# The third 2-byte part of q and k: from a product with minus the identity on TensorE to a subtraction on GpSimd

## The chip, the cores and the metric

The kernel runs on one core of a Trainium2 chip. The metric is the device time of one execution in microseconds (us); lower is better. The kernel before takes 673.02 us, the median of three runs (672.89 to 673.35). PE stands for TensorE, DVE for VectorE, ACT for ScalarE, POOL for GpSimd, SP for SyncE, the engine whose queue issues most DMAs.

## What is computed

Two independent computations stand side by side in one output of 2048 x 1152. Half A is attention with a compressive memory over a 2048 x 576 input, 32 heads of 18, in four segments of 512 rows. Half B filters another 2048 x 576 input in the frequency domain.

```python
# half A
q, k, v = heads(x @ wq), heads(x @ wk), heads(x @ wv)      # 32 heads of 18, N = 4 segments of L = 512
for s in range(4):
    p = softmax(qs @ ks.T * scale + causal_mask)
    a_mem = (phi(qs) @ M) / (phi(qs) @ z + 1e-6)           # phi(t) = t + 1 if t > 0 else exp(t)
    outs.append(g * a_mem + (1 - g) * (p @ vs))
    M, z = M + phi(ks).T @ vs, z + phi(ks).sum(rows)
a = concat(outs) @ wo
# half B
b = irfft2(rfft2(x) * (w_r + 1j * w_i))
```

All of it is 4-byte arithmetic in the reference. The kernel gets near that on TensorE by splitting an operand into a high part and the remainder; for the scores of the attention it holds each of q and k as a sum of three 2-byte numbers.

## The kernel before

Four stages follow one another on TensorE: the forward transform of half B (to about 67 us), the projections of half A (about 67 to 274 us), the inverse transform of half B (about 274 to 347 us), and the attention. The middle of half B, its small transforms across slices and its multiplication by the filter, is elementwise work on DVE. It is cut into steps of one instruction or half an instruction, and a pacer issues a given number of these steps between the pieces of the projections (`pace.take`). There is no scheduler that reorders: every engine runs its instructions in the order in which the code issues them, and waits at each for its inputs and its buffers.

**The projections** (`projections`) run over the four segments g. Each segment has 13 units: nine units of q and k (`qk_unit`, mt = 0 to 8, here q0 to q8; mt < 4 holds q rows, mt = 4 a mixture, mt > 4 k rows) and four of v (`v_unit`, v0 to v3). A q unit is 14 products of 128x128 by 128x512 into one PSUM bank named `pj` (L487). A v unit is two banks of 14 products with 288 columns; in the first three segments five small products per v unit (`pm`), issued some steps later, add up the memory matrix. The tag `pj` has five banks, shared by both kinds. A unit is a generator: its passes are issued in its own turn of the loop, and its later steps in the turns of the units behind it, two steps in each turn (`advance`), the older unit first.

**The steps of a q unit**, after its passes, with the lines of the kernel before:

1. ACT writes the first 2-byte part `sp3[:,j0]` from `pj` (L500). Where phi is needed, ACT also makes exp(min(t,0)) in tile `ex` (L503, L504).
2. DVE makes phi in `ex` (L506, with one operand in PSUM and one in SBUF), and subtracts the first part from `pj` in place (L507).
3. ACT writes the second part from `pj` (L514).
4. PE multiplies minus the identity (`nid`, 2-byte) with the second part and adds it to `pj` (L516): what is left in the bank is the third part, which ACT copies out (L517). SP stores the three parts to DRAM (L520, L521; for mt = 4 six DMAs, L526), and PE transposes phi of k (L533).
5. ACT copies the transposes into `pk` (L536, L537).

Step 1 of a unit stands right behind step 3 of the unit before it in ACT's order, so that per unit ACT runs L514, L500, L503, L504, L517. The tile `sp3` has three buffers; L500 of a unit waits until the stores of the third unit before it have landed. `vt`, the tile of 622 columns into which ACT copies v (L551), has two buffers; POOL writes its columns of ones (L548, L549), SP stores it (L552), and `pm` reads it (L559).

**DVE's other work there**: the steps of half B (L232, L244, L267, L270, L274, L276), which read two operands from SBUF and write SBUF, the remainders of the inputs and weights (L431, L460, L466), which do too, and the masking of the memory matrix from PSUM (L567). In the last segment DVE also makes the split `Y` (L305) of the first two units of the inverse transform, of which the first products after the projections (L320) read. POOL does little in this stage: memsets, the sums of the memory matrix (L572 to L576), and in the last segment the issue of the DMAs for the tables of the inverse transform (L285, L286, L291), which waits until the last q unit has released the weights.

Of the kernel before, what the change touches and what calls it, by code (L numbers as in the profile page):

```python
# [5 lines left out]
F32=mybir.dt.float32; F32R=mybir.dt.float32r  # L6
AF=mybir.ActivationFunctionType; OP=mybir.AluOpType
# [358 lines left out]
BF=mybir.dt.bfloat16  # L366
# [43 lines left out]
class ATT:  # L410
# [78 lines left out]
    def qk_unit(s,g,mt,tp,pp):  # L489

        nc=s.nc
        ps=pp.tile([128,512],F32,name="pj",tag="pj")
        yield from s.passes(ps,g,"wqk",slice(128*mt,128*mt+128),slice(0,512),False)
        yield
        sp3=tp.tile([128,3,512],BF,name="sp3",bufs=3)
        r0=0 if (g>0 or mt>4) else 64
        r1=128 if (g<3 or mt<4) else 64
        if (g==0 and mt<4) or (g==3 and mt>4): r1=r0
        j=[2,1,0] if mt>4 else [0,2,1] if mt<4 else [0,1,2]
        nc.scalar.copy(sp3[:,j[0]],ps)  # L500
        if r1>r0:
            e=tp.tile([128,512],F32,name="ex")
            nc.scalar.activation(e[r0:r1],ps[r0:r1],AF.Relu,scale=-1.0)  # L503
            nc.scalar.activation(e[r0:r1],e[r0:r1],AF.Exp,scale=-1.0)  # L504
        yield
        if r1>r0: nc.vector.scalar_tensor_tensor(e[r0:r1],ps[r0:r1],0.0,e[r0:r1],op0=OP.max,op1=OP.add)  # L506
        nc.vector.tensor_tensor(ps,ps,sp3[:,j[0]],op=OP.subtract)  # L507
        qr=min(r1,128 if mt<4 else (64 if mt==4 else 0))
        if qr>r0:
            a=s.pqD[g][0]  # L510
            J=[(18*8*mt*512,[[512,16],[18*512,8]],e[:qr])] if mt<4 else [((16+j)*512,[[18*512,32]],e[32*j:32*j+32]) for j in range(2)]
            for o,ap,x in J: nc.sync.dma_start(bass.AP(tensor=a.tensor,offset=a.offset+o,ap=ap+[[1,512]]),x)
        yield
        nc.scalar.copy(sp3[:,j[1]],ps)  # L514
        yield
        nc.tensor.matmul(ps,s.nid,sp3[:,j[1]],start=False,stop=True,skip_group_check=True)  # L516
        nc.scalar.copy(sp3[:,j[2]],ps)  # L517
        if mt!=4:
            d=s.qkD[g][mt-(mt>4)]; o=mt<4
            nc.sync.dma_start(d[o:o+3].rearrange("i p c -> p i c"),sp3)  # L520
            nc.sync.dma_start(d[3-3*o],sp3[:,1-o])  # L521
        else:
            for r,i,c,n in ((0,0,1,3),(0,1,1,2),(0,2,1,1),(64,0,3,3),(64,0,2,2),(64,0,1,1)):
                m={3:0,2:3,1:5}[n]; a=s.reD[g][r*12//64+2*m]
                x=sp3[r:r+64,i:i+c] if c==n else sp3[r:r+64,i:i+1].to_broadcast([64,n,512])
                nc.sync.dma_start(bass.AP(tensor=a.tensor,offset=a.offset,ap=[[512,64],[64*512,n],[1,512]]),x)  # L526
        if r1<=r0: return
        k0=max(r0,0 if mt>4 else (64 if mt==4 else 128))
        if k0>=r1: return
        n=r1-k0  # L530
        pt=pp.tile([128,4,128],F32,name="ptr",tag="pt")
        for tb in range(4):
            nc.tensor.transpose(pt[:,tb,:n],e[k0:r1,128*tb:128*tb+128],s.ident[k0:r1,k0:r1])  # L533
        yield
        pk=s.pk.rearrange("p a (h d) -> p a h d",d=18)
        if mt==4: nc.scalar.copy(pk[:,:,:,16:],pt[:,:,:n].rearrange("p a (d h) -> p a h d",d=2))  # L536
        else: nc.scalar.copy(pk[:,:,8*mt-40:8*mt-32,:16],pt.rearrange("p a (d h) -> p a h d",h=8))  # L537
    def v_unit(s,g,tb,tp,pp):
        nc=s.nc
        P=[]  # L540
# [36 lines left out]
    def projections(s,xp,tp,pp,wv,pace,hook):  # L577

        live=[]
        s.nid=wv.tile([128,128],BF,name="nid"); s.nc.scalar.activation(s.nid,s.ident,AF.Copy,scale=-1.0)  # L580
        lw=s.load_w("wv",576,wv,xp,288,"xl",4)
        def advance():
            for l in list(live):
                try: next(l)
                except StopIteration: live.remove(l)
        tot=pace.left-8
        for g in range(4):
            if g<3: xq=[s.xprep(g+1,t,(xp,s.x0)[g%2],xp,[128,512],"xst",2) for t in range(5)]
            for i in range(13):
                u=s.qk_unit(g,i,tp,pp) if i<9 else s.v_unit(g,i-9,tp,pp)  # L590
                if i==4 and g<3: s.pk=tp.tile([128,4,576],F32,name="pk",bufs=1)
                next(u)
                hook(g,i)
                next(lw,None); next(lw,None)
                if g<3 and i in (4,6,8,10,12): next(xq[(i-4)//2])
                if g<3 and i in (1,3,5,7,9): next(xq[(i-1)//2])
                w=tot/(35+13*2.4+3*1.6)*((1.0 if i<9 else 2.4 if g<3 or i<10 else 1.6) if g>0 or i>0 else 0.0)
                advance()
                pace.take(w*.4)
                advance()  # L600
                next(u)
                pace.take(w*.6)
                live.append(u)
        while live: advance()
# [595 lines left out]
```

## Time and profile before

| what | value |
|---|---|
| time, median of 3 runs | 673.02 us |
| the profiled execution's own time | 673.47 us |
| its span | 671.8 us |
| busy over the span | PE 658.6 us (98%), DVE 543.2 (81%), ACT 440.6 (66%), POOL 189.6 (28%) |
| granted TensorE clock | 1.00 |
| projections (about 67 to 274 us) | PE busy throughout but for some 0.6 us |

A row of a timeline gives the start, the duration, the engine, the line, and in brackets the idle time before it with what ended that. A row of a group gives the total busy time and the mean of one. A busy PE is not PE at its peak: its products overlap, so what one of them costs is read from start to start. A row of the windows gives, for each stretch, its length and then the busy time of PE, PE's weight loads, DVE, ACT and POOL, with the number of instructions.

### The profile page before, as it was taken

The numbers are of one execution on the slowest core, as the hardware profiler recorded it, in microseconds if no ns is written. First come the engines' busy times: TensorE is split into PE (matmuls) and PEld (weight loads), VectorE is DVE, ScalarE is ACT, GpSimd is POOL, SyncE is SP. The second block draws the span as 40 slices with busy tenths as digits, with TensorE's granted clock in tenths as the row PEclk, the third lists the DMA queues.
The fourth block names the chain that finished last, engine by engine and source line by source line (L and its number), as shares of the span: only waits on it lengthen the run. The fifth ranks groups of instructions, "written<-read, shape, count | busy, mean of one in ns | idle before, by whom it ended". The sixth has DMA issues, their size and how long they took to land.

```text
span 671.8 us, 14143 instructions
## 1 busy us (share of the span) xinstructions
PE 658.6 (98%) x4776; PEld 484.3 (72%) x4776; DVE 543.2 (81%) x1514; ACT 440.6 (66%) x900; POOL 189.6 (28%) x387
## 2 busy tenths in 40 slices
PE   9999999999999999999999999999999999998997
PEld 5999779879879878999974454444666445663597
DVE  5998989889889778689769998998856988568643
ACT  3886796576487385444449988878756787567521
POOL 2111000100200012456506543445323564133410
PEclk9999999999999999999999999999999999999999
DMA  9896466497388478799545885876667576332152
GB/s 339 306 310 195 124 185 206 143 300 233 89 239 266 132 231 266 223 264 289 168 134 157 219 218 152 204 219 182 166 165 204 135 200 161 99 113 79 35 171 75
DMA packets 76034, 127.57 MB, mean 190 GB/s; under 512 B 12812, under 2 KB 44202, under 8 KB 72370
## 3 DMA queue, kind: packets, MB, share of 16 engines
q1 hardware_dynamic: 69310, 110.67, 57.3%
q0 software_dynamic: 5632, 15.76, 8.2%
q8 instruction: 37, 0.61, 0.4%
q10 hardware_dynamic: 1020, 0.25, 0.2%
q14 instruction: 35, 0.29, 0.1%
HBM read 81.78 MB, written 43.92 MB: 187 GB/s over the span
## 4 chain that ended last, share of the span: by engine, by line
PE 86%; DVE 5%; ACT 3%; DMA 3%; issue 2%; POOL 1%; SPq 0%; ACTq 0%; DVEq 0%; POOLq 0%
PE pj L487 15%; PE pv L763 11%; PE s L688 10%; PE pjv L487 7%; PE po L916 5%; PE i L331 4%; PE i L320 4%; PE f L145 4%; PE s L725 4%; PE c L166 4%; PE s L729 3%; PE pn L837 2%; PE s L735 2%; PE po L946 2%; PE pm L559 2%
## 5 line engine op out<-in xcount | busy, mean ns | idle before, releaser
L692 DVE CUSTOM_DVE_ANT_0 junk<-s,x 128x384 bf16<-128x384 f32 (+3 forms) x512 | 219.1, 486 | 42.2 <-PE s L688 39.7
L738 POOL TENSOR_SCALAR_AFFINE_SELECT P<-P 128x512 f32<-128x512 f32 (+2 forms) x135 | 80.6, 620 | 51.6 <-ACT P L726 47.3
L726 ACT ACTIVATE P<-s 128x512 f32<-128x512 f32 x128 | 76.7, 599 | 20.6 <-PE s L725 17.6
L763 PE MATMUL pv<-P,vs 128*32 128x512 f32 (+3 forms) x1024 | 81.0, 438 | 0.0
L731 ACT ACTIVATE P<-s 128x512 f32<-128x512 f32 x128 | 76.2, 596 | 3.4 <-PE s L730 3.0
L763 PEld LDWEIGHTS pv<-P,vs 128*32 128x32 f32 x1024 | 27.2, 109 | 44.0 <-issue 39.9
L688 PE MATMUL s<-Ks,Qs 108*128 108x512 bf16 (+3 forms) x256 | 57.7, 300 | 1.0 <-DVE mg L692 0.4
L487 PE MATMUL pj<-x,wqkh 128*128 128x512 f32 x162 | 56.1, 408 | 0.0
L232 DVE TENSOR_TENSOR Z<-Z 128x580 f32<-128x580 f32 (+2 forms) x51 | 45.9, 913 | 0.6
L692 DVE DVE_READ_ACCUMULATOR2_ANT mg<- 128x1 f32 x512 | 42.5, 83 | 0.0
L548 POOL MEMSET vt<- 128x32 f32 x16 | 2.3, 162 | 139.3 <-PE pm L559 125.5
L320 PE MATMUL i<-civ,Y 128*128 128x256 f32 (+1 forms) x288 | 39.7, 290 | 0.9 <-POOL Y L305 0.9
L736 ACT ACTIVATE P<-s 128x512 f32<-128x512 f32 x64 | 38.7, 605 | 2.5 <-PE s L735 1.1
L688 PEld LDWEIGHTS <-Qs 108*128 108x128 bf16 x320 | 26.9, 98 | 15.6 <-issue 11.0
L320 PEld LDWEIGHTS i<-civ,Y 128*128 128x128 f32 (+1 forms) x288 | 36.8, 181 | 1.9 <-POOL Y L305 1.3
L331 PE MATMUL i<-itab,T 128*128 128x290 f32 (+1 forms) x224 | 36.0, 304 | 0.1
L487 PE MATMUL pj<-x,wqkl 128*128 128x512 f32 x90 | 35.5, 395 | 0.0
L487 PE MATMUL pj<-xh,wqkh 128*128 128x512 f32 x90 | 35.5, 395 | 0.0
L487 PE MATMUL pj<-xh,wqkl 128*128 128x512 f32 x90 | 35.5, 395 | 0.0
L487 PEld LDWEIGHTS pj<-x,wqkh 128*128 128x128 f32 x162 | 30.5, 189 | 6.4
L506 DVE SCALAR_TENSOR_TENSOR ex<-pj,ex 128x512 f32<-128x512 f32 (+1 forms) x28 | 19.3, 689 | 19.5 <-ACT ex L504 19.4
L514 ACT CAST sp<-pj 128x512 bf16<-128x512 f32 x36 | 21.1, 585 | 18.6 <-DVE pj L507 18.4
(209 smaller groups left out, 1694.1 us busy)
## 6 DMA issues: line engine op xcount, KB each, us to landing
qkD<-sp SPq DMA_DIRECT2D x32, 384.0 KB
xin<-xb SPq DMA_DIRECT2D x16, 384.0 KB
cfw<-cfw POOLq DMA_DIRECT2D x16, 384.0 KB, 4.8
civ<-civ POOLq DMA_DIRECT2D x16, 384.0 KB, 8.3
Ks<-qkD SPq DMA_DIRECT2D x12, 512.0 KB
x<-qkD SPq DMA_DIRECT2D x10, 512.0 KB
Qs<-qkD SPq DMA_DIRECT2D x10, 512.0 KB
vs<-vD SPq DMA_DIRECT2D x16, 310.5 KB
```

Of the source, the lines that this page charges most:

```text
L232: s.nc.vector.tensor_tensor(o,a,b,op=op)
L320: nc.tensor.matmul(p[:m,k],Y[i][:,q,c*128:c*128+m],cc[:,hl,o:o+256],start=n==0,stop=n==5)
L331: nc.tensor.matmul(p,x,t,start=n==0,stop=n==6)
L487: s.nc.tensor.matmul(out,a,b,start=i==0,stop=i==len(L)-1)
L688: for o,i,e in J: nc.tensor.matmul(p[:,o:o+128*i+128],Q[:108,h+e,128*i:128*i+128],K[:108,h+e,:128*(i+1)],start=True,stop=True)
L692: nc.vector.tensor_tensor_reduce(out=junk[:,:w],in0=p[:,o:o+w],in1=s.mask[:,512-w:],scale=1.0,scalar=-3.0e38, op0=OP.add,op1=OP.max,accum_ ...
L726: nc.scalar.activation(P[0][:,hh],p0,AF.Exp,scale=SC)
L731: nc.scalar.activation(P[1][:,hh],p1,AF.Exp,scale=SC)
L736: nc.scalar.activation(P[2][:,hh-1:hh+1].rearrange("p h c -> p (h c)"),p2,AF.Exp,scale=SC)
L738: nc.gpsimd.affine_select(out=x[:,a:b],in_=x[:,a:b],pattern=[[0,b-a],[1,128]],compare_op=OP.is_ge,fill=0.0,base=0,channel_multiplier=-1)
L763: nc.tensor.matmul(s.pvt[32*hh:32*hh+32,128*j:],vt[:,152*j+19*h:152*j+19*h+32],mv[0][:,hh,mv[1]],start=j==0,stop=j>1,skip_group_check=True)
L916: nc.tensor.matmul(ps,a[t][:r,c],b[:r,t,w],start=i==0,stop=i==13)
```

## The change

In `qk_unit` the difference of step 2 goes to SBUF instead of back into PSUM: DVE writes it as `d1`, 512 of the 622 columns of a buffer of the tag `vt`. ACT makes the second part from `d1`. The third part is no longer made by PE and ACT: POOL subtracts the second part from `d1` and writes the 2-byte result into `sp3`. The product with `nid` and the third copy of ACT fall away, and so does the making of `nid`. A `pj` bank is now released after DVE's subtraction. The transposes stay where they were in PE's order; ACT's copy into `pk` and its step stay too, but the stores of `sp3` are issued one step later, behind that copy.

```diff
-        nc.vector.tensor_tensor(ps,ps,sp3[:,j[0]],op=OP.subtract)
+        d1=tp.tile([128,622],F32,name="vt")[:,:512]
+        nc.vector.tensor_tensor(d1,ps,sp3[:,j[0]],op=OP.subtract)
...
         yield
-        nc.scalar.copy(sp3[:,j[1]],ps)
-        yield
-        nc.tensor.matmul(ps,s.nid,sp3[:,j[1]],start=False,stop=True,skip_group_check=True)
-        nc.scalar.copy(sp3[:,j[2]],ps)
+        nc.scalar.copy(sp3[:,j[1]],d1)
+        yield
+        nc.gpsimd.tensor_tensor(sp3[:,j[2]],d1,sp3[:,j[1]],op=OP.subtract)
+        k0=max(r0,0 if mt>4 else (64 if mt==4 else 128)); n=r1-k0
+        if n>0:
+            pt=pp.tile([128,4,128],F32,name="ptr",tag="pt")
+            for tb in range(4):
+                nc.tensor.transpose(pt[:,tb,:n],e[k0:r1,128*tb:128*tb+128],s.ident[k0:r1,k0:r1])
+        yield
+        if n>0:
+            pk=s.pk.rearrange("p a (h d) -> p a h d",d=18)
+            if mt==4: nc.scalar.copy(pk[:,:,:,16:],pt[:,:,:n].rearrange("p a (d h) -> p a h d",d=2))
+            else: nc.scalar.copy(pk[:,:,8*mt-40:8*mt-32,:16],pt.rearrange("p a (d h) -> p a h d",h=8))
         if mt!=4:
             d=s.qkD[g][mt-(mt>4)]; o=mt<4
             nc.sync.dma_start(d[o:o+3].rearrange("i p c -> p i c"),sp3)
...
-        if r1<=r0: return
-        k0=max(r0,0 if mt>4 else (64 if mt==4 else 128))
-        if k0>=r1: return
-        n=r1-k0
-        pt=pp.tile([128,4,128],F32,name="ptr",tag="pt")
...
-        s.nid=wv.tile([128,128],BF,name="nid"); s.nc.scalar.activation(s.nid,s.ident,AF.Copy,scale=-1.0)
```

In PE's order, in the first segment, the product of q0 stood in the middle of the passes of q2. Before:

```order
L487 MATMUL pj<-x_838,wqkl 128x512
L487 MATMUL pj<-x_838,wqkh 128x512
L516 LDWEIGHTS nid
L516 MATMUL pj<-sp_1012,nid 128x512
L487 MATMUL pj<-x_838,wqkh 128x512
L487 MATMUL pj<-x_838,wqkl 128x512
```

36 such pairs, four segments of nine, are gone, and the passes follow one another there. On ACT, in the second segment (`sp` is sp3), one unit before:

```order
L514 CAST sp_1657<-pj 128x512
L500 CAST sp_1691<-pj 128x512
L503 ACTIVATE ex<-pj 128x512
L504 ACTIVATE ex<-ex 128x512
L517 CAST sp_1657<-pj 128x512
```

and the same unit now:

```order
L515 CAST sp_1656<-vt 128x512
L500 CAST sp_1690<-pj 128x512
L503 ACTIVATE ex<-pj 128x512
L504 ACTIVATE ex<-ex 128x512
L515 CAST sp_1690<-vt 128x512
```

The first four instructions stand as before and the fifth, the third copy, is gone. On POOL, towards the end of the q units of the first segment, only the memsets of `vt` (L548, L549) stood before; now the order reads:

```order
L517 TENSOR_TENSOR sp_1235<-vt,sp_1235 128x512
L517 TENSOR_TENSOR sp_1274<-vt,sp_1274 128x512
L547 MEMSET vt 128x32
L548 MEMSET vt 128x14
L517 TENSOR_TENSOR sp_1324<-vt,sp_1324 128x512
L547 MEMSET vt 128x32
L548 MEMSET vt 128x14
```

Each q unit has put one subtraction there. DVE's order is the same as before, but that its subtraction (now L508) writes `vt`; in the second segment, from the subtraction of q2 to that of q4, it reads now:

```order
L508 TENSOR_TENSOR vt<-pj,sp_1656 128x512
L276 TENSOR_TENSOR Z<-Z,T 128x2x290
L460 TENSOR_TENSOR x_1684<-xst,x_1684 128x512
L267 TENSOR_TENSOR T<-Z,W 128x1160
L506 SCALAR_TENSOR_TENSOR ex<-pj,ex 128x512
L508 TENSOR_TENSOR vt<-pj,sp_1690 128x512
L270 TENSOR_TENSOR Z<-Z,W 128x2x580
L506 SCALAR_TENSOR_TENSOR ex<-pj,ex 128x512
L508 TENSOR_TENSOR vt<-pj,sp_1726 128x512
```

Nothing moved here against the rows of before, where L507 stands in the place of L508: between two subtractions there are three steps of other work in one unit and a single one in the next.

More of the change, by code (lines that the diff above doesn't have):

```diff
@@ L526, in qk_unit @@
                 nc.sync.dma_start(bass.AP(tensor=a.tensor,offset=a.offset,ap=[[512,64],[64*512,n],[1,512]]),x)
-        if r1<=r0: return
-        k0=max(r0,0 if mt>4 else (64 if mt==4 else 128))
-        if k0>=r1: return
-        n=r1-k0
-        pt=pp.tile([128,4,128],F32,name="ptr",tag="pt")
-        for tb in range(4):
-            nc.tensor.transpose(pt[:,tb,:n],e[k0:r1,128*tb:128*tb+128],s.ident[k0:r1,k0:r1])
-        yield
-        pk=s.pk.rearrange("p a (h d) -> p a h d",d=18)
-        if mt==4: nc.scalar.copy(pk[:,:,:,16:],pt[:,:,:n].rearrange("p a (d h) -> p a h d",d=2))
-        else: nc.scalar.copy(pk[:,:,8*mt-40:8*mt-32,:16],pt.rearrange("p a (d h) -> p a h d",h=8))
     def v_unit(s,g,tb,tp,pp):
```

## Prediction

> **What bounds the kernel now.** I read the busy time by stretches first, one stretch for each segment of the projections and the last cut off where DVE has finished what the inverse transform waits for. The columns behind the length are PE, PE's weight loads, DVE, ACT, POOL.
>
> ```profile
> 76.00:129.00 53.00, 53.00 (x310) 45.22 (x309) 47.08 (x69) 38.10 (x84) 1.56 (x11) 1.00 0.62 185
> 129.00:182.00 53.00, 53.00 (x310) 45.30 (x309) 46.29 (x58) 35.23 (x71) 3.79 (x20) 1.00 0.68 210
> 182.00:235.00 53.00, 53.00 (x310) 45.24 (x308) 46.09 (x55) 32.92 (x65) 2.38 (x13) 1.00 0.72 208
> 235.00:271.00 36.00, 35.39 (x191) 29.67 (x191) 29.65 (x45) 22.98 (x50) 5.66 (x19) 1.00 0.84 256
> ```
>
> PE never stops: 53.00 of 53.00 us, three times. So PE bounds the stage, and what leaves PE's order can shorten it. But DVE stands close behind: it is busy for 47.08 + 46.29 + 46.09 + 29.65 = 169.1 of 195 us, which leaves 25.9 us of idle time. POOL is nearly empty. The question is whether the work put on POOL stays off DVE.
>
> **What PE gains.** The start times show what a product with minus the identity costs, since the ends overlap.
>
> ```profile
> 184.88 0.40 PE L487 MATMUL pj<-x,wqkl 128*128 128x512 f32 x1
> 185.12 0.40 PE L487 MATMUL pj<-x,wqkh 128*128 128x512 f32 x1
> 185.35 0.39 PE L516 MATMUL pj<-sp,nid 128*128 128x512 bf16 x1
> 185.40 0.58 PE L487 MATMUL pj<-x,wqkh 128*128 128x512 f32 x1
> 185.81 0.39 PE L487 MATMUL pj<-x,wqkl 128*128 128x512 f32 x1
> ...
> PE pj L516 <- ACT sp L514: 0.6, 2, 0.3
> ```
>
> A pass follows the other after 0.23 to 0.24 us. With L516 between, two passes take 185.81 - 185.12 = 0.69 instead of 0.47 us: 0.22 us for one L516, not the 0.39 of its row. 36 of them make 7.9 us, and PE's two waits for ACT in front of L516 another 0.6: 8.5 us. PE's own path would end the projections 8.5 us earlier.
>
> **What POOL's subtraction costs.** A subtraction of this size on POOL is in the trace, in the inverse transform. What it does to DVE is seen where both work from SBUF, near the end of the kernel. First three groups, then DVE's and POOL's timeline there.
>
> ```profile
> L305 POOL TENSOR_TENSOR Y<-Z,Y 128x512 fp32r<-128x512 f32 x14 | 16.6, 1187 | 21.4 <-ACT Y L304 21.4
> L793 POOL TENSOR_TENSOR ry<-ry,rw 128x128 f32<-128x128 f32 x8 | 3.7, 463 | 18.8 <-ACT rw L792 15.4 <-DMA x<-qkD 3.4
> L794 POOL CAST rw<-ry 128x128 bf16<-128x128 f32 x8 | 2.7, 332 | 0.5
> ...
> 647.04 0.69 DVE L928 TENSOR_TENSOR ux<-ux,am 126x512 f32<-126x512 f32 x1
> 647.65 0.92 DVE L933 TENSOR_TENSOR P<-ux,P 126x512 fp32r<-126x512 f32 x1
> ...
> 647.31 0.70 POOL L793 TENSOR_TENSOR ry<-ry,rw 128x128 f32<-128x128 f32 x1 [12.56 <-ACT rw L792]
> 648.08 0.63 POOL L794 CAST rw<-ry 128x128 bf16<-128x128 f32 x1
> ```
>
> L928 and L933 are the same operation in size, with both operands in SBUF, back to back. L793 arrives at 647.31 while L928 runs. It takes 0.70 instead of its 0.46 and ends 0.28 us after L928: it was held until then. L933, next on DVE, takes 0.92 instead of 0.69: it was held by L793. And L794, behind it, is held by L933 (0.63 against 0.33). So the two engines take turns, whoever waits comes next, and DVE loses the length of POOL's operation less about 0.23 us (0.46 - 0.23 = 0.23). For a subtraction of 1.19 us that is 0.96 us per turn.
>
> The rule is also in the Trainium skill ("SBUF — State Buffer", section "Who interferes with whom"): a DVE instruction with two SBUF inputs contends with a GpSimd instruction that reads SBUF, and the second one to issue is blocked until the first has finished. The trace agrees that they exclude each other. By the page the loss would be the whole 1.19 us, 0.23 more in each turn than the rows give; with the 23 turns counted below, 5.3 us more in the sum.
>
> A DVE operation with an operand in PSUM isn't held; L352 takes 0.69 beside POOL's L305 as it does alone:
>
> ```profile
> 280.71 1.85 POOL L305 TENSOR_TENSOR Y<-Z,Y 128x512 fp32r<-128x512 f32 x2
> ...
> 281.98 0.69 DVE L352 TENSOR_TENSOR T<-i,T 128x512 fp32r<-128x512 f32 x1 [1.32 <-ACT T L350]
> ```
>
> So L506 and the subtraction L508 run free. The rest of DVE's work here (L232, L244, L267 to L276, L431, L460) reads two operands from SBUF and can be held.
>
> **How often DVE is held.** These are two q units of the second segment on DVE, then ACT in the second of them.
>
> ```profile
> 133.49 0.69 DVE L507 TENSOR_TENSOR pj<-pj,sp 128x512 f32<-128x512 f32 x1
> 134.09 0.75 DVE L276 TENSOR_TENSOR Z<-Z,T 128x580 f32<-128x580 f32 x1
> 134.76 0.68 DVE L460 TENSOR_TENSOR x<-xst,x 128x512 fp32r<-128x512 f32 x1
> 135.36 1.36 DVE L267 TENSOR_TENSOR T<-Z,W 128x1160 f32<-128x1160 f32 x1
> 136.64 0.68 DVE L506 SCALAR_TENSOR_TENSOR ex<-pj,ex 128x512 f32<-128x512 f32 x1
> 137.24 0.69 DVE L507 TENSOR_TENSOR pj<-pj,sp 128x512 f32<-128x512 f32 x1
> 137.83 1.36 DVE L270 TENSOR_TENSOR Z<-Z,W 128x1160 f32<-128x1160 f32 x1
> 140.34 0.69 DVE L506 SCALAR_TENSOR_TENSOR ex<-pj,ex 128x512 f32<-128x512 f32 x1 [1.15 <-ACT ex L504]
> ...
> 137.96 0.58 ACT L514 CAST sp<-pj 128x512 bf16<-128x512 f32 x1 [1.03 <-DVE pj L507]
> 138.45 0.59 ACT L500 CAST sp<-pj 128x512 bf16<-128x512 f32 x1
> 139.04 0.60 ACT L503 ACTIVATE ex<-pj 128x512 f32<-128x512 f32 x1
> 139.67 0.63 ACT L504 ACTIVATE ex<-ex 128x512 f32<-128x512 f32 x1
> ```
>
> ACT's second part ends 0.6 us after DVE's subtraction, and POOL's subtraction asks then. In the first unit L276 is over by that time and L460 has just begun; POOL waits for it, and L267 waits for POOL: 0.96 us. In the second unit POOL waits for L270, and behind it comes L506, which is free: DVE loses nothing, since it waits 1.15 us for ACT there anyway. So a unit costs DVE 0.96 us if another SBUF step stands behind the one that POOL waits for, before L506. Counted in this way over DVE's order: 8 of 9 units in the first segment, 6 in the second, 5 in the third, 4 in the fourth with the fractions (POOL's sums of the memory matrix push the first unit's subtraction under later steps). 23 turns, 22.1 us. Nothing (if DVE were never held) and 36 x 1.19 = 42.8 us (each unit, whole) are the ends; the count stands between, and the time of a turn is from the nearest row.
>
> **How much idle time takes it up.** 25.9 us are there, but not all can be used. From L507 to the next L506 ACT must do L514, L500, L503, L504 (137.96 to 140.30), whatever the change takes from ACT behind them, so that a unit with one step stays at 3.6 us. I count one such unit in the first segment, two in the second, two and a half in the third and three in the fourth, with about 1.1 us each; 0.5 us of small gaps in each of the first two; DVE's waits for POOL's sums, 1 us in each of the last two; and in the fourth 1 us in which L500 of q7 waits for the six stores of q4, which then come later as well. Together 1.6 + 2.7 + 3.8 + 5.3 = 13.4 us stay. What goes is the idle time at the start of each segment, where DVE waits for PE's passes (three rows; behind them DVE's wait for POOL's sums as the third segment begins):
>
> ```profile
> 124.92 0.69 DVE L506 SCALAR_TENSOR_TENSOR ex<-pj,ex 128x512 f32<-128x512 f32 x1 [1.85 <-ACT ex L504]
> 177.86 0.69 DVE L506 SCALAR_TENSOR_TENSOR ex<-pj,ex 128x512 f32<-128x512 f32 x1 [1.55 <-ACT ex L504]
> 230.80 0.69 DVE L506 SCALAR_TENSOR_TENSOR ex<-pj,ex 128x512 f32<-128x512 f32 x1 [3.19 <-ACT ex L504]
> ...
> DVE mm L567 <- POOL zst L576: 1.0, 3, 0.5
> ```
>
> There and in units with many steps 25.9 - 13.4 = 12.5 us are taken up. DVE's path to the second split `Y` grows by 22.1 - 12.5 = 9.6 us.
>
> **The end of the stage** decides what that is worth.
>
> ```profile
> 260.69 0.69 DVE L507 TENSOR_TENSOR pj<-pj,sp 128x512 f32<-128x512 f32 x1
> ...
> 270.06 1.08 DVE L305 TENSOR_TENSOR Y<-Z,Y 128x512 fp32r<-128x512 f32 x2
> ...
> 273.89 5.04 PE L320 MATMUL i<-civ,Y 128*128 128x256 f32 x40
> ...
> 281.88 2.04 PE L331 MATMUL i<-itab,T 128*128 128x290 f32 x14
> ```
>
> Before, the second `Y` is ready at 271.1 and PE begins the inverse transform at 273.9. Then it would be ready at 271.1 + 9.6 = 280.7. 36 products L320 still follow it (two units of 18, at 5.04 / 40 = 0.126 us: 4.5 us) before the first L331; with 0.7 us allowed for waits on the splits between them it starts at 285.9, 4.0 us later than the 281.9 of before. PE alone would be there 8.5 us early, but it cannot run that far ahead: five `pj` banks let it be about three units in front of DVE, and v2 needs the bank that the subtraction of q8 releases (260.7 + 9.6 less its own turn of 0.96 = 269.3, and 0.7 for itself). Two v units of 28 passes, at little more than the 0.126 us of L320 for 288 columns against 256 (an estimate: 0.13, so 7.3 us), and the 18 products of the first inverse unit (2.3 us) end at 279.6: PE waits for DVE's second `Y`, if only just. From L331 on PE is full as before, and the 4.0 us stay. In the profiled execution's terms 673.5 + 4.0 = 677.5 us; it stands 0.45 above the median, so 677.0 us.
>
> **Parts that cost nothing or little.** DVE's subtraction into SBUF instead of PSUM: L352 (PSUM and SBUF in, SBUF out) takes the same 0.69. The `vt` buffers: each waits for POOL's subtraction two units back, done by then. At a segment's start the first two wait for the landing of v; with DVE late, that is over. ACT loses 36 copies of 0.57 us behind its chain, which nobody waits for. The stores now stand behind `pk`'s copy and, in SP's order, behind loads of the filter `W` that wait for L270: where DVE is late they are late, and L500 three units on may wait 1 to 2 us; I put this at nothing, and in the range at up to 3 us in all.
>
> **The rivals.** (a) *PE's path stays the longest.* If POOL got its turn only under L506 and L508, 1.3 us of free work for its 1.19, DVE would lose nothing, and the time would be 673.0 - 8.5 = 664.5 us. For it: PE's full rows. Against it: L793 got in between L928 and L933. 12%. (b) *Held, but shorter.* Faster than before where the turns cost DVE less than 22.1 - 4.0 = 18.1 us, 0.79 us each or 19 turns of 0.96. The place is the step behind POOL's subtraction in the q units of the first two segments, with 14 of the 23. With 0.6 us a turn the sum is 4.0 - 8.3 = -4.3, 669 us. 13%, and 13% that it ends within 0.2% (1.3 us, about what a measurement of this kernel can tell) of no change. (c) *Slower still*: the whole 1.19 us a turn and late stores, 4.0 + 5.3 + 3 = 12.3 us, 685 us. 12%. (d) *The product was hidden on PE*: excluded by the 0.69 us in start times.
>
> **How the numbers follow.** The forecast, DVE bound with 2 to 9 us more, has 50%; with (c), slower has 62%, faster 25% with (a) and (b), the same 13%. The range takes in DVE's turns from 0.45 to 1.19 us: 667 to 682.5 us; half of (c) and most of (a) are left out.
>
> **What would show it.** Right: L517 of about 1.2 us with many of 1.5 to 2.5 (held); of L232 to L276 in q units some at 1.7 or 2.3 us instead of 0.76 or 1.36; DVE nearly without idle time at the three segment starts; PE waiting for a `pj` bank in late segments and for `Y` before the first L320; the second pair of L305 near 281. Wrong: L232 at 0.76 us throughout, or PE at L320 near 265 us without a wait.

## The result, and the profile after

The kernel after takes 693.92 us (median of 6 runs, 692.98 to 697.05), the kernel before on the same chip 673.18 us (6 runs, 672.89 to 674.05). The ratio is 1.0313, 95% interval 1.0291 to 1.0336: 3.1% slower. The profiled execution of after took 693.23 us, with a span of 691.2 us and a granted clock of 0.988. The forecast was 677.0 us: the sign was right, the loss five times too small.

The lines of after that the readings below speak of: L506 phi, L508 the difference `d1`, L515 the second part, L517 POOL's subtraction, L522 the transposes, L526 and L527 `pk`, L530 and L531 the stores of `sp3` (L536 for the fifth unit), L513 the stores of phi of q (`pqD`), L550 v's copy, L551 v's store.

The first view is the same table by stretches as in the prediction (PE, weight loads, DVE, ACT, POOL), the last stretch now up to the second split `Y`. Behind the instruction counts stand granted clock, DMA share and GB/s.

```profile
76.00:129.00 53.00, 46.80 (x266) 40.71 (x265) 50.56 (x63) 31.21 (x69) 15.81 (x19) 0.97 0.58 176
129.00:182.00 53.00, 47.29 (x260) 40.30 (x260) 42.56 (x48) 28.03 (x53) 17.06 (x25) 0.97 0.64 201
182.00:235.00 53.00, 50.92 (x286) 44.10 (x285) 49.45 (x56) 29.95 (x59) 19.76 (x25) 0.97 0.60 183
235.00:289.40 54.40, 51.13 (x294) 44.92 (x292) 48.55 (x63) 24.93 (x53) 20.77 (x35) 1.00 0.77 232
```

PE, full before, now stops for 6.2, 5.7 and 2.1 us in the first three. DVE is busy 191.1 us up to the second `Y` instead of 169.3: 21.8 us more, against 22.1 forecast. But it is also idle for 213.4 - 191.1 = 22.3 us, where 13.4 were forecast. The groups show who is held (the numbers behind the first bar: total in us, mean of one in ns). First the three DVE groups before, then POOL's and the same three after:

```profile
L232 DVE TENSOR_TENSOR Z<-Z 128x580 f32<-128x580 f32 x18 | 13.4, 758 | 0.2
L270 DVE TENSOR_TENSOR Z<-Z,W 128x1160 f32<-128x1160 f32 x8 | 10.9, 1364 | 0.2
L460 DVE TENSOR_TENSOR xl<-xst,xh 128x512 fp32r<-128x512 f32 x8 | 5.5, 685 | 0.1
...
L517 POOL TENSOR_TENSOR sp<-vt,sp 128x512 bf16<-128x512 f32 x36 | 58.7, 1630 | 86.1 <-ACT sp L515 78.4 <-DMA reD<-sp 5.6 <-DMA xst<-xa 2.0
L232 DVE TENSOR_TENSOR Z<-Z 128x580 f32<-128x580 f32 x19 | 16.9, 902 | 0.2
L270 DVE TENSOR_TENSOR Z<-Z,W 128x1160 f32<-128x1160 f32 x8 | 13.7, 1708 | 0.2
L460 DVE TENSOR_TENSOR xl<-xst,xh 128x512 fp32r<-128x512 f32 x8 | 8.4, 1045 | 0.1
```

So the turns are there in the forecast size. In DVE's timeline up to the second `Y`, 22 steps are longer by 0.85 to 1.0 us: 7, 6, 5 and 4 in the four segments, where 8, 6, 5 and 4 were counted; five more are longer by 0.2 to 0.6 us. What is new is in the waits up to the second `Y` (us in all, times, longest):

```profile
DVE ex L506 <- ACT ex L504: 17.2, 12, 3.3
ACT sp L500 <- DMA qkD<-sp: 12.3, 7, 3.4
PE ptr L522 <- DVE ex L506: 10.3, 7, 2.3
...
ACT sp L500 <- DMA reD<-sp: 2.3, 1, 2.3
```

L500 waits 14.6 us in all for stores of the third unit before its own; before it was 2.2:

```profile
ACT sp L500 <- DMA reD<-sp: 1.8, 1, 1.8
ACT sp L500 <- DMA qkD<-sp: 0.4, 1, 0.4
```

The reason is seen in SP's order in the second segment; the DVE, POOL and ACT rows belong to it:

```profile
137.04 0.54 SPq L513 DMA_DIRECT2D pqD<-ex  x1
139.11 0.81 SPq L257 DMA_DIRECT2D W<-w  x2
139.98 0.42 SPq L454 DMA_DIRECT2D xst<-xa  x1
140.50 0.38 SPq L530 DMA_DIRECT2D qkD<-sp  x1
...
137.53 1.55 DVE L270 TENSOR_TENSOR Z<-Z,W 128x1160 f32<-128x1160 f32 x1
...
136.70 1.17 POOL L517 TENSOR_TENSOR sp<-vt,sp 128x512 bf16<-128x512 f32 x1
...
145.39 0.59 ACT L500 CAST sp<-pj 128x512 bf16<-128x512 f32 x1 [2.80 <-DMA qkD<-sp]
```

The third part is ready at 136.70 + 1.17 = 137.87, but its store is issued at 140.50. It stands behind a load of `W` that needs a buffer which DVE's L270 releases at 137.53 + 1.55 = 139.08. It lands late, L500 of the third unit on waits until 145.39, and DVE waits for phi behind it.

At the end of the stage (DVE, ACT, PE, PE):

```profile
288.26 1.08 DVE L305 TENSOR_TENSOR Y<-Z,Y 128x512 fp32r<-128x512 f32 x2
...
290.09 0.70 ACT L550 COPY vt<-pjv 128x288 f32<-128x288 f32 x2 [1.67 <-DMA vD<-vt]
...
290.85 8.89 PE L320 MATMUL i<-civ,Y 128*128 128x256 f32 x54 [4.51 <-ACT vt L550]
299.58 2.04 PE L331 MATMUL i<-itab,T 128*128 128x290 f32 x14
```

The second `Y` is ready at 289.3, 18.2 us later than before, not 9.6. PE does nothing for 4.51 us and then starts the first product of the inverse transform not behind `Y`, but behind the copy of v3 (290.09 + 0.70). Before, 40 of these products ran in one go from 273.89, and the copy of v3 began only at 276.15:

```profile
276.15 0.70 ACT L551 COPY vt<-pjv 128x288 f32<-128x288 f32 x2 [2.77 <-DMA vD<-vt]
```

The first L331 comes 10.2 us behind `Y`, not 5.2.

The theory from the traces: three causes, the held turns (T), the late stores (L), and what stands in front of the first L320 and L331 (the end). The rival: only one of them counts, and the others are waits that move over to each other.

### The profile page after: what moved, and what is told of

It reads as the page before. It is cut to its first block, busy times and chain, and to the rows that moved or that the text cites. A ratio compares the mean times of both kernels' runs of the same rounds, so it can differ in the third digit from the quotient of the medians.

```text
span 691.2 us, 14129 instructions
## 1 busy us (share of the span) xinstructions
PE 659.6 (95%) x4740; PEld 487.9 (71%) x4740; DVE 564.9 (82%) x1514; ACT 424.4 (61%) x863; POOL 248.9 (36%) x423
## 4 chain that ended last, share of the span: by engine, by line
PE 62%; DVE 13%; DMA 8%; issue 6%; ACT 6%; POOL 2%; SPq 2%; ACTq 0%; DVEq 0%; POOLq 0%
PE s L686 10%; PE pv L761 10%; PE i L320 5%; PE po L914 5%; PE i L331 4%; PE s L723 4%; PE f L145 4%; DVE Z L232 3%; PE c L166 3%; PE pj L487 3%; PE s L727 3%; PE pjv L487 2%; DMA qkD<-sp 2%; PE pn L835 2%; PE s L733 2%
## 5 line engine op out<-in xcount | busy, mean ns | idle before, releaser
L517 POOL TENSOR_TENSOR sp<-vt,sp 128x512 bf16<-128x512 f32 x36 | 58.7, 1630 | 86.1 <-ACT sp L515 78.4
L232 DVE TENSOR_TENSOR Z<-Z 128x580 f32<-128x580 f32 (+2 forms) x51 | 50.0, 993 | 0.5
L515 ACT CAST sp<-vt 128x512 bf16<-128x512 f32 x36 | 22.3, 620 | 44.0 <-DVE vt L508 44.0
L320 PE MATMUL i<-civ,Y 128*128 128x256 f32 (+1 forms) x288 | 41.4, 300 | 4.5 <-ACT vt L550 4.5
L320 PEld LDWEIGHTS i<-civ,Y 128*128 128x128 f32 (+1 forms) x288 | 38.8, 192 | 5.3 <-ACT vt L550 4.7
L703 POOL CAST mh<-mg 128x16 bf16<-128x16 f32 x31 | 6.2, 199 | 87.6 <-DVE mg L690 55.4
L500 ACT CAST sp<-pj 128x512 bf16<-128x512 f32 x36 | 21.0, 582 | 26.1 <-DMA qkD<-sp 12.3
```

The source lines that it names most:

```text
L232: s.nc.vector.tensor_tensor(o,a,b,op=op)
L320: nc.tensor.matmul(p[:m,k],Y[i][:,q,c*128:c*128+m],cc[:,hl,o:o+256],start=n==0,stop=n==5)
L517: nc.gpsimd.tensor_tensor(sp3[:,j[2]],d1,sp3[:,j[1]],op=OP.subtract)
```

## The experiments

### A square: turns and stores

First the stores alone: in after, moved up one step, right behind POOL's subtraction.

```diff
         nc.gpsimd.tensor_tensor(sp3[:,j[2]],d1,sp3[:,j[1]],op=OP.subtract)
+        (stores of sp3)
         k0=...; transposes
         yield
         pk copies
-        (stores of sp3)
```

> The kernel after, with the stores of sp3 issued in the step of POOL's subtraction, right behind it, instead of one step later behind the transposes and pk's copy; all else as after. Theory L (late stores): the stores stood in SP's order behind loads of W and pq stores that wait for DVE, so L500 waited for sp3 and DVE behind it; here ACT's waits for DMA qkD and reD in front of L500 fall from 14.6 us to under 3, DVE's idle time from 76 us to the second Y falls from 22.3 to about 13.4 us, and the time is 693.9 - 8.9 = 685 us (683 to 688). Rival H (only the held turns count: with DVE late anyway, the waits for stores just go over into waits for DVE's phi): the same waits move to other instructions, DVE's idle time stays above 19 us, 691 to 694 us.

Measured: 687.24 us, ratio to before 1.0193 (1.0177 to 1.0208); 6.7 us gained. The waits for stores up to the second `Y`, ready at 284.0:

```profile
ACT sp L500 <- DMA reD<-sp: 2.3, 1, 2.3
ACT sp L500 <- DMA qkD<-sp: 1.5, 1, 1.5
```

14.6 us have become 3.8, DVE's idle time 17.0 us (22.3 before the edit). Theory L holds: the time is inside its range (683 to 688), but the gain is less than the 8.9 us that it gave.

Then the turns alone: POOL writes the third part without reading anything. The memset is also shorter than the subtraction (0.52 us), does not wait for ACT's second part and frees the buffer of `d1` earlier, so this edit takes away more than POOL's reads.

```diff
-        nc.gpsimd.tensor_tensor(sp3[:,j[2]],d1,sp3[:,j[1]],op=OP.subtract)
+        nc.gpsimd.memset(sp3[:,j[2]],0.0)
```

> The kernel after, with POOL writing zeros into the third part of q and k (a memset of 128x512 bf16 elements) in the place of the subtraction: the third part is left out of the result, and POOL reads nothing from SBUF at this place. Everything else, buffers, orders and stores, is as after. Theory T (DVE is held in turns by POOL's reads of SBUF): DVE's busy time from 76 us to the second Y falls back by about 21.8 us to 169 us, L232 Z<-Z to 0.76 us; with DVE early its loads of W come early and so do the stores; the time falls to 665 to 673 us. Rival P (the time was lost to the later stores, to transposes that wait for phi and to v's buffers, DVE's longer steps being a bystander): 685 to 693 us. Rival W (POOL's access of SBUF holds DVE whether it reads or writes): DVE's steps stay long, 685 to 693 us.

Measured: 685.95 us, 1.0167 (1.0135 to 1.0199). DVE's groups, then the waits:

```profile
L232 DVE TENSOR_TENSOR Z<-Z 128x580 f32<-128x580 f32 x18 | 13.4, 757 | 0.2
L270 DVE TENSOR_TENSOR Z<-Z,W 128x1160 f32<-128x1160 f32 x8 | 10.9, 1363 | 0.2
...
DVE ex L506 <- ACT ex L504: 27.6, 21, 3.8
ACT sp L500 <- DMA qkD<-sp: 21.2, 10, 6.6
```

The turns are gone to within 1 ns of before, so rival W falls: POOL holds DVE by what it reads. That is what the Trainium skill says ("SBUF — State Buffer", "Who interferes with whom": a GpSimd instruction that only writes SBUF does not contend with a DVE instruction of two SBUF inputs). But theory T as it was put falls too: DVE is busy only 168.9 us and the time is still 686 us, since L500 now waits 21.2 us for stores. That is the range of rival P, by way of the stores. What the turns released, the late stores took.

The late stores in the kernel before. The added step also moves PE's transposes and the copy into `pk` of the same unit one step later, which after leaves in place, so this is not the stores alone:

```diff
         nc.scalar.copy(sp3[:,j[2]],ps)
+        yield
         (stores of sp3)
```

> The kernel before, with the product with minus the identity and all else in place, but the stores of sp3 issued one step later, as in after. Theory L (late stores cost by themselves, through L500 which needs the buffer of three units back): ACT's waits for DMA qkD and reD in front of L500 rise from 2.2 us to 15 to 22 us, as in the run with the memset, DVE waits for ACT, and the time rises to 680 to 688 us though no operation is added anywhere. Rival D (stores are late only where DVE is late, and DVE is not late here): 673 to 676 us.

Measured: 687.09 us, 1.0207 (1.0189 to 1.0226). No operation is added, DVE is not held, and the time rises by 13.7 us. L500's waits for stores are again those of after:

```profile
ACT sp L500 <- DMA qkD<-sp: 15.2, 9, 3.6
ACT sp L500 <- DMA reD<-sp: 0.4, 1, 0.4
```

The fourth corner, both edits of after together:

> The kernel after with both the memset in place of POOL's subtraction (the third part of q and k is zero, left out of the result) and the stores of sp3 in the step of that memset. It is the fourth corner of a square: held and late (after, 693.9), held and early (687.2), free and late (686.0), and this one, free and early. Theory T and L together (two causes that stand in for each other: each alone is enough to make DVE's path the longest): with both gone DVE is busy 169 us, L500 waits under 3 us for stores, and PE's path is the longest again: 673.7 - 8.5 = 665 us (664 to 668). Rival A (the two add like terms): 686.0 - 6.7 = 679 us. Rival O (something else of the change, transposes or v's buffers, keeps PE back): 670 to 676 us with PE waiting in front of the transposes or of v.

Measured: 670.08 us, 0.9949 (0.9929 to 0.9970).

| | stores late | stores early |
|---|---|---|
| DVE held in turns | 693.9 (after) | 687.2 |
| DVE free (memset) | 686.0 | 670.1 |

In the square only the stores move from one column to the other, not the transposes. From the corner without either, the turns alone cost 17 us, the late stores alone 16, both 24. They do not add: each uses up the same slack in front of DVE's path. That is why undoing one of them gains only 7 or 8 us. The corner is also 5 us slower than its forecast of 665, in the range of rival O and with the sign that it named: PE has lost its products, but stops for v3's copy in front of L320; the end of the stage comes back below.

```profile
270.46 8.29 PE L320 MATMUL i<-civ,Y 128*128 128x256 f32 x54 [2.69 <-ACT vt L550]
```

### What makes a late store costly

The run with late stores in the kernel before, with the stores issued from ACT's queue instead of SP's (all but those of the fifth unit):

```diff
 # the kernel before with late stores, and
-            nc.sync.dma_start(d[o:o+3]..., sp3); nc.sync.dma_start(d[3-3*o], sp3[:,1-o])
+            nc.scalar.dma_start(d[o:o+3]..., sp3); nc.scalar.dma_start(d[3-3*o], sp3[:,1-o])
```

> The kernel before with the stores of sp3 one step later (687.1 us), but those of all units except the fifth issued from ACT's queue instead of SP's. They are still one step late, but no longer stand behind pq stores and loads of W and x that wait for DVE. Theory S (what makes a late store costly is SP's order): ACT's waits for DMA qkD in front of L500 fall from 15.2 us to under 4 us and the time is back at 673 to 677 us. Rival (one step late is too late whatever the queue, since the buffer of three units back is needed): 683 to 688 us.

Measured: 678.92 us, 1.0069 (1.0048 to 1.0091). ACT's waits for `qkD` fall from 15.2 to 1.5 us, and 8.2 of the 13.7 us are gone, though the stores are as late in the program as there. So most of it is SP's order. The forecast was 673 to 677 us; for the 5 us that stay, a control with the stores in their old step on ACT's queue:

> The kernel before with the stores of sp3 at their old step, but issued from ACT's queue (all units except the fifth). It is the control for the run with late stores on ACT's queue (678.9 us). If the 5 us that stayed there are the price of issuing from ACT, this gives 677 to 680 us; if they are the price of the one step, 672 to 674.5 us.

Measured: 686.46 us, 1.0193 (1.0178 to 1.0209), neither of the two. Issuing a pair takes 0.38 and 0.50 us on ACT between L517 and the next cast (138.90 to 139.81 in its timeline), so this control has a cost of its own and tells nothing of the step. The 5 us stay open; the transposes, one step later in the run before it, are a cause that no run here parts from the rest.

### A turn against the same time as DVE's own work

```diff
 # the kernel before, and
-        nc.tensor.matmul(ps,s.nid,sp3[:,j[1]],start=False,stop=True,skip_group_check=True)
-        nc.scalar.copy(sp3[:,j[2]],ps)
+        nc.vector.tensor_tensor(sp3[:,j[2]],ps,sp3[:,j[1]],op=OP.subtract)
...
-        s.nid=wv.tile([128,128],BF,name="nid"); s.nc.scalar.activation(s.nid,s.ident,AF.Copy,scale=-1.0)
```

> The kernel before, with DVE subtracting the second part from PSUM for the third part (128x512, PSUM and SBUF in, bf16 out) in the place of the product with minus the identity and of ACT's copy; nothing on POOL, stores where they were. DVE gets 36 operations of 0.6 us, 21.6 us, as much as the held turns of after (21.8 us), and no turns. Theory T (what POOL's subtraction costs DVE is time on DVE, nothing else): the time is that of the run with the subtraction on POOL and early stores, 687 us (684 to 690), with DVE busy 191 us from 76 us to the second Y. Forecast's sum (13.4 us of DVE's idle time stays): 677 us. Rival: POOL's subtraction costs more than its turns (clock, later transposes), then this is clearly under 684 us.

Measured: 674.44 us, 1.0018 (1.0007 to 1.0030). DVE is busy 189.9 us up to its second `Y`, as with the turns, but idle only 9.4 us instead of 17.0, so the theory that a turn is time on DVE and nothing else (687 us) falls. The same unit of the second segment, first with DVE's own operation, then with POOL's turns and early stores:

```profile
143.00 0.68 DVE L516 TENSOR_TENSOR sp<-pj,sp 128x512 bf16<-128x512 f32 x1
144.12 0.69 DVE L506 SCALAR_TENSOR_TENSOR ex<-pj,ex 128x512 f32<-128x512 f32 x1 [0.44 <-ACT ex L504]
```

```profile
142.82 2.33 DVE L267 TENSOR_TENSOR T<-Z,W 128x1160 f32<-128x1160 f32 x1
...
148.69 0.69 DVE L506 SCALAR_TENSOR_TENSOR ex<-pj,ex 128x512 f32<-128x512 f32 x1 [1.06 <-ACT ex L504]
```

DVE's operation stands at the end of a unit and goes into the gap in front of phi; a turn falls on a long step elsewhere (L267 takes 2.33 us instead of 1.36) and the gap of 1.06 stays. As these kernels differ in more than that, one with the engine alone changed:

```diff
 # after with early stores, and
-        nc.gpsimd.tensor_tensor(sp3[:,j[2]],d1,sp3[:,j[1]],op=OP.subtract)
+        nc.vector.tensor_tensor(sp3[:,j[2]],d1,sp3[:,j[1]],op=OP.subtract)
```

> The kernel with early stores (687.2 us) with one word changed: DVE instead of POOL computes the third part, from the same difference in SBUF, at the same place of the program. Buffers, transposes and stores stay as they are there. Theory G (a turn costs more than the same time spent as an operation of DVE's own, because a turn falls on long steps and DVE's own 0.6 us falls into gaps of about 1 us in front of phi): DVE is busy about 190 us, its idle time falls from 17 to about 9 us, 675 us (673 to 677), as with DVE subtracting from PSUM (674.4). Rival B (transposes one step later, vt and the rest of the new order cost the 13 us, not POOL): 684 to 688 us.

Measured: 678.58 us, 1.0075 (1.0058 to 1.0092). From 687.2 to 678.6: 8.7 us are POOL's turns against DVE's own work. The forecast was 673 to 677 us; the other 4.1 us, against DVE's subtraction in the old order, are the rest of the new order. DVE's second `Y` is ready at 274.7 here and at 275.3 with the old order, but the first L331 follows it by 10.5 us instead of 7.5: in these profiles the loss lies at the end of the stage. (The profiled execution with the old order took 676.54 us, 2.1 above its median.)

### The end of the stage

Two edits that take v's buffers out of the way: `d1` of the units without phi goes into the buffers of `ex`, and v2 and v3 of the last segment into that of `pk`.

```diff
-        d1=tp.tile([128,622],F32,name="vt")[:,:512]
+        d1=tp.tile([128,622],F32,name="vt")[:,:512] if r1>r0 else tp.tile([128,512],F32,name="ex")
 # and in the third run, in v_unit
-        vt=tp.tile([128,622],F32,name="vt")
+        vt=(half of the buffer of pk) if g==3 and tb>1 else tp.tile([128,622],F32,name="vt")
```

> The kernel after, with the difference d1 of the units without phi (q of the first and k of the last segment) in the buffers of ex, which those units do not use, so that v0 and v1 of the last segment do not wait for POOL's subtractions of the last k units; all else as after. Theory V (the end of the stage is set by v's buffers): the landing of v1, 7.9 us on the chain that ended last, begins earlier, v3's copy L550 no longer stands in front of the inverse transform, the first L331 starts at Y + 5.2 instead of Y + 10.4 us, and the time is 693.9 - 5.2 = 689 us (687.5 to 690.5). Rival: the end is set by DVE's second Y and by PE's 54 products behind it alone, and v3's wait is a bystander: 692.5 to 694.5 us.

> Both edits: stores of sp3 with POOL's subtraction, and d1 of units without phi in the buffers of ex. If late stores (8.9 us) and v's buffers (5.2 us) are two causes on one chain, they add: 693.9 - 14.1 = 680 us (677 to 683), and what is left over before is the 4 us that the held turns were forecast to cost plus about 2 us behind L331. If only one of them counts, the time is that of the better of the two alone (685 or 689 us). If neither, 692 to 694 us.

> The kernel with early stores and d1 of units without phi in the buffers of ex (686.4 us), and v2 and v3 of the last segment in the buffer of pk, which is free by then, so that their copies do not wait for the landing of v0 and v1. Theory B (the beginning of the inverse transform is set by v's copies, which wait for landings of about 7 us): ACT's waits for DMA vD, 8.8 us, go, the first L320 does not wait for v3, the first L331 comes at Y + 5.2 instead of Y + 9.0 us, and the time is 686.4 - 3.8 = 682.6 us (681.5 to 684). Rival: DVE's second Y and PE's 54 products behind it set it whatever v does: 685.5 to 687 us.

Measured: 691.22 us (1.0276, 1.0235 to 1.0317) with the first edit alone, 686.35 (1.0182, 1.0163 to 1.0201) with it beside the early stores, and 685.50 (1.0187, 1.0158 to 1.0216) with both beside the early stores. The first gains 2.7 us of the 5.2 forecast, but its interval overlaps that of after (1.0291 to 1.0336); beside the early stores the medians fall by 0.9 and again 0.9 us. These runs tell none of the three gains from nothing, and the forecasts of 680 and 682.6 us were missed. The profile of the third run is of an execution of 688.78 us, 3.3 above its median. In it PE waits only 0.49 us for v's copy (L553 there), but stops a little later (PE, then DVE):

```profile
281.95 4.51 PE L320 MATMUL i<-civ,Y 128*128 128x256 f32 x36 [0.49 <-ACT pk L553]
290.04 4.18 PE L320 MATMUL i<-civ,Y 128*128 128x256 f32 x18 [3.58 <-issue]
...
284.40 3.22 DVE L232 TENSOR_TENSOR Z<-Z 128x580 f32<-128x580 f32 x3
287.65 1.69 DVE L232 TENSOR_TENSOR Z<-t 128x580 f32<-128x580 f32 x2
289.26 0.68 DVE L352 TENSOR_TENSOR T<-i,T 128x512 fp32r<-128x512 f32 x1
```

The profile names no releaser for the 3.58 us. By the code the third unit's products need a bank that DVE's L352 of the first unit releases, and L352 stands behind 4.9 us of DVE's own steps that follow `Y`: PE goes on at 290.04, just after L352 ends (289.94). So in that execution v's landing is one of two things that are late.

A third suspect was the PSUM bank: the first L320 in the new order waits for v3's copy, in the kernel before it did not. Three unused accumulators, taken first, move those of L320 to other banks:

```diff
+                    for t in ("i3","i3","mt"): pi.tile([128,512],F32,name="pad",tag=t)
```

> The kernel with DVE in POOL's place in the new order (678.6 us), with the accumulators of the inverse transform laid on other PSUM banks: three unused tiles taken first, so that the first unit of L320 no longer shares a bank with v3 and does not wait for v3's copy. Theory K (in the new order the first products behind the projections sit on v3's bank, and v3's copy waits for the landing of v1): PE's wait in front of L320, 3.2 us, goes, the first 18 products and the clock are gained, and the time is 675 to 677 us, near the 674.4 of DVE's subtraction in the old order. Rival (DVE's own steps behind the second Y set L331 whatever the banks): 678 to 679 us.

> The kernel with POOL's subtraction and early stores (687.2 us) with the same shift of banks. Theory K: the first L331 comes at Y + 7 to 8 us instead of Y + 10.1, the time is 684.5 us (683.5 to 686). Rival (DVE's steps behind Y): 686.5 to 688 us.

Measured: 675.30 us (1.0032, 1.0020 to 1.0044) and 684.41 us (1.0160, 1.0146 to 1.0174): 3.3 and 2.8 us gained by banks alone. With POOL's subtraction, without the shift and with it:

```profile
285.19 9.20 PE L320 MATMUL i<-civ,Y 128*128 128x256 f32 x54 [4.19 <-ACT vt L550]
```

```profile
279.94 2.30 PE L320 MATMUL i<-civ,Y 128*128 128x256 f32 x18
284.22 6.20 PE L320 MATMUL i<-civ,Y 128*128 128x256 f32 x36 [1.98 <-ACT vt L550]
290.26 2.04 PE L331 MATMUL i<-itab,T 128*128 128x290 f32 x14
```

18 products run ahead, and L331 comes 7.2 us behind `Y` (283.1) instead of 10.2. Of the 4.1 us that the new order cost without POOL, 3.3 were this.

### Versions for use

Units in which DVE waits for ACT anyway should take the subtraction free of charge; the others keep the product. POOL in 11 units, DVE in 14, DVE in 22, and the 14 with the shift of banks:

```diff
+        if (g,mt) in FREE: (subtraction by POOL from d1, or by DVE from pj)
+        else: product with minus the identity and ACT's copy, as before
```

> The kernel before, in which 11 of the 36 units take the change (difference into SBUF, third part by POOL, stores in the same step): units in which one DVE step stands between the subtraction and the next phi, so that POOL's turn falls where DVE waits for ACT anyway. The other 25 keep the product. Theory T: the turns cost DVE next to nothing, PE loses 11 x 0.22 = 2.4 us, the time is 671 us (670 to 672.5). Rival: the end of the stage (v's landing, DVE's T splits) holds PE whatever it gains: 673 to 674 us; or turns cost anyway: 675 to 678 us.

> The kernel before, in which DVE takes the third part from PSUM in 14 of the 36 units: those before whose next phi DVE waits 0.37 to 1.95 us for ACT. The other 22 keep the product and ACT's copy. Theory G (a DVE step of 0.6 us in a gap of about 1 us is free): DVE's second Y is not later than before, PE loses 14 x 0.22 = 3.1 us, the time is 670.3 us (669.5 to 672). Rival (the end of the stage holds PE): 673 to 674 us.

> As the run with 14 units on DVE, with 8 more in the first two segments, where DVE waits 1.5 to 1.9 us for PE as the next segment begins. Theory G: most of the 8 x 0.6 = 4.8 us goes into that idle time, PE loses 22 x 0.22 = 4.8 us, the time is 669 us (668 to 671). Rival (DVE has become the bound, as with all 36 units on it at 674.4 us): 671 to 674 us.

> The kernel with DVE taking the third part in 14 units (672.15 us) with the same shift of banks. PE was 94 to 99 per cent busy up to the first L320 there, so theory K gives it little: 671.5 us (670.5 to 672.5). If its end too was held by v3's copy, 669 to 670 us.

Measured: 672.82 us (0.9986, 0.9971 to 1.0000), 672.15 (0.9979, 0.9965 to 0.9992), 673.13 (0.9991, 0.9980 to 1.0002) and 671.62 (0.9978, 0.9964 to 0.9992). The second and the fourth beat the kernel before, by 0.2%. The first two gain less than was forecast (671 and 670.3 us) and the third comes out in its rival's range; what took the rest is not shown. The single runs scatter from 669.98 to 674.65 us, so the half microsecond between them is not shown. With 22 units DVE is late again (its last L305 starts at 272.9, with 14 at 269.1).

## Why the prediction was wrong, point by point

In the profiled execution the forecast was 677.5 us, and 693.2 was measured; the 15.7 us between them come apart as follows. The step that failed most is the one that put the late stores at nothing (point 4); the path from the second `Y` to the first L331 (point 6) and the idle time that stays (point 3) were taken too short as well. The cost of the turns, which the forecast was built on, was right.

1. *PE gains 8.5 us on its own path.* Borne out on PE's path, but not in the time: in the run with the memset and early stores the last pass of v3 starts at 267.47 instead of 273.76, 6.3 us earlier, and PE was idle for 2.1 us before it, 8.4 us together. Only 3.3 us came through, since PE then stopped for v3's copy.
2. *POOL and DVE take turns, 23 of 0.96 us, 22.1 us.* Right: 21.8 us, the 22 long turns lie in the forecast segments, and the memset took them away whole. The Trainium skill's rule that the second to issue is blocked ("SBUF — State Buffer", "Who interferes with whom") holds; by its whole 1.19 us a turn it would have been 5.3 us more, which the sum does not show.
3. *13.4 us of DVE's idle time stay.* Mis-sized: 17.0 us stay with early stores. The gaps of about 1 us stay as forecast; the idle time at the start of the second segment, which was to be used up, grew (the first L506 there waits 3.35 us with early stores, 1.85 before; ACT waits for PE's passes, so PE is late by then). `Y` would be ready at 284.0 instead of 280.7: 3.3 us.
4. *The late stores, put at nothing and in the range at up to 3 us.* This step failed worst. The mechanism was named, and even its way (behind loads of `W` that wait for L270); its price was not worked out. One step in the program is half a unit, and SP's order puts the next unit's `pqD` store and loads of `W` and x between; the store and the load of `W` wait for DVE. In after it costs 5.3 us at the second `Y` (289.3 against 284.0) and 6.7 us in time; without the turns, between the two memset kernels, 15.9 us. The prediction did not price the cover: three buffers of `sp3` are three units, and L500 already waited for stores before (2.2 us).
5. *PE runs three units ahead of DVE in five banks.* Wrong: PE's transposes stand in its order and wait for phi (10.3 us in after), while its waits for a bank that DVE holds come to 0.2 us. What this costs by itself was not tried.
6. *The first L331 at `Y` + 5.2 us.* It came at `Y` + 10.2: 5.0 us. 3.0 of them are the bank that L320 shares with v3 in the new order (10.2 to 7.2 with the shift, measured with early stores). The forecast let 18 products run ahead of `Y`; in after none did. For the rest the rows show two things, without an edit that parts them: DVE's own steps behind `Y`, and the clock, below.
7. *The `vt` buffers, put at nothing.* 2.7 us where the stores are late, about 1 us where they are early; neither is clear of the noise, so nothing here refutes it.
8. *From L331 on nothing changes.* From there to the end the profiled executions take 393.7 us against 391.6. The profiled runs here have 391 to 395 without order, so these 2.1 us are not put down to anything.

3.3 + 5.3 + 5.0 + 2.1 = 15.7 us. Rival (c), held with late stores, 685 us, was the right kind, but took its late stores at 3 us, and reached its size partly by the whole 1.19 us a turn, which did not come. Of the signs named in advance, held L517 and held L232 to L276 came as said. PE did stop before the first L320, but for v3's copy and not for `Y`, and hardly for a `pj` bank; the second pair of L305 came at 288.3, not near 281; "DVE nearly without idle time" did not come, and was the sign that the turns were not all. The lower end of the range does not follow from its own premise either: with turns of 0.45 us the sum is 677.0 - 23 x 0.51 = 665.3 us, not 667.

## What to carry to other kernels

When an edit moves a DMA issue by one step, list what stands ahead of it in the issuing queue at its new place and what each of those waits for; the delay is the longest of these waits, not the step. Price a buffer's cover (so many units ahead) against that delay before putting it at nothing. Time that one engine took from another by contention was worse here than the same time as an operation placed by hand, which could go into the gaps (8.7 us). Two delays on one path can hide each other: undone singly they gained 7 and 8 us here, together 24.

## What the runs showed of the hardware

- POOL's memset of 128x512 2-byte elements (0.52 us each) beside DVE's operations with two SBUF operands leaves these at 757 and 1363 ns; POOL's subtraction, which reads SBUF, raises them to 902 and 1708 ns.
- A short stop of PE costs clock afterwards. In after, behind a stop of 4.51 us (stretch, PE, weight loads, DVE, ACT, POOL, then granted clock, DMA share and GB/s):

```profile
290.80:295.00 4.20, 4.15 (x19) 4.16 (x20) 2.65 (x5) 1.07 (x2) 0.00 (x0) 0.50 0.48 119
```

  The granted clock is 0.50 over these 4.2 us, and 54 products take 8.89 us, where 40 took 5.04 before (0.165 against 0.126 us each: 2.1 us at most, since the third unit's products also need a split on POOL, which ends at 297.34). Behind the stop of 2.69 us in the run with memset and early stores it is 0.58 over the next 4.1 us. The Trainium skill describes it ("TensorE: Matmul & The Clock Gate", "Part 1: The HAM clock gate": half speed after about 3.4 us of idle time, until about 3.4 us of activity); the trace agrees on the half speed behind the longer stop, and shows it behind one of 2.69 us as well.
- Which PSUM bank the first tile of the next stage falls on was worth 2.8 to 3.3 us, with no operation of the kernel changed.
